# Fused attention and expert block: q in one transfer, 64x64 score tiles, scale chains in PSUM, transposed output, a re-planned order

## The chip, the cores and the metric

One Trainium2 chip, one of its cores. The metric is the device time of the program in microseconds (us), median of three runs. Five engines appear: TensorE (PE for matmuls, PEld for weight loads), VectorE (DVE), ScalarE (ACT), GpSimd (POOL) and SyncE (SP), which issues the transfers.

## The reference

Causal attention over 4 batches of 12 heads, 448 positions, head size 64, then an expert layer with three hidden projections and a maximum over them:

```python
scores = scale * np.matmul(q, k.transpose(0, 1, 3, 2))
scores = np.where(mask, -1000000000.0, scores)
attn = np.exp(scores - max); attn = attn / (sum + 1e-09)
x = np.matmul(attn, v)            # laid out as [4 * 448, 768]
h = np.maximum(np.maximum(x @ w1, x @ w2), x @ w3)
out = h @ w_out                   # [1792, 768], all float32
```

## The kernel before

**Precision.** Score matmuls run in float32. Everything behind them runs in float16 as a high and a low part (`hi`, `lo`), three matmuls per product. The weights arrive as 64-bit floats and are turned into such pairs on the chip.

**Order.** Nothing is issued as written. Functions record operations with `add`, each with engines it may run on, a cost, what it reads and writes, a priority and a ring of buffers; `Order.forward` (L127) places them greedily in planned time, and `Order.run` emits them in that order. So each engine's queue is a fixed list, and an instruction whose data is late holds up all behind it. `W_AT` (L31) says when each of 24 weight tiles is due, `V_AHEAD` when values are loaded. PE has no allowance: an instruction may be planned for the moment at which its data is planned to be ready.

**Attention.** A unit is a pair of heads; there are 24, six per batch. `staging` (L433) loads k as [128, 448] and q as [128, 512] in three transfers: 384 columns, and for the last 64 queries two blocks of 64x64 on the diagonal of a 128x128 square whose rest was set to zero at the start (L866). The tile is scaled by 0.125. `attend` (L453) makes scores in two halves, each in a PSUM tile S (two tiles exist). The first half holds queries 256 to 383 and 0 to 127. The second (from L476) holds 128 to 255 and the last 64 queries of both heads: mask matmuls, then two matmuls over all 128 rows with the zero-padded square as stationary operand (L480, L481; 256 and 192 columns), then two matmuls of 64 rows each, one per head. Row maxima are taken by DVE (L497), exponentials by ACT (L508). The first six pairs ("plain") multiply float32 probabilities with v after PE transposes (L522, L595) and divide at the end (`quotient`, L623). The other 18 scale and split p into halves (L308, L319), transpose them by DMA (L562) and multiply with split v (L582).

**Weights.** `weight` (L655) loads a 768 KB tile, takes the absolute value on ACT (L696), the largest entry (L681) and three bit steps (L685, L689, L693) on DVE; `scales` (L702) makes power-of-two factors for three tiles at a time: `all_max` (L337) spreads the maxima over partitions with a PE matmul into one of three PSUM tiles M, DVE reduces them into `wpm` in SBUF (L347), and four small DVE instructions follow on SBUF tiles (L712, L354, L357, L719). `values` has the same chain once per batch for v. `split` (L730) writes the float16 pair, high part on ACT, POOL or DVE, low part on DVE (L328) or POOL.

**Expert layer.** `hidden` (L765): per batch and per 128 hidden columns, three groups of 18 matmuls of 448 columns (L779), scaled and combined on ACT and DVE (L793), split again. `project` (L816): output rows of 128 tokens by 384 columns, 18 matmuls each with h as stationary operand (L825). The 64 tokens left over per batch are copied by POOL into `hL` (L809), and two batches share a group. There are 28 groups.

The lines of the second half's scores, for the two places that change most:

```python
m(256, 256, qq[:, 384:512], kk[:, 0:256])      # L480
m(768, 192, qq[:, 384:512], kk[:, 256:448])    # L481
```

Of the kernel before, what the change touches and what calls it, by code (L numbers as in the profile page):

```python
# [15 lines left out]
P = 128  # L16
D = 64
# [13 lines left out]
W_AT = [1.0, 1.2, 1.39, 0.71, 0.9, 1.1, 3.11, 3.31, 3.51, 2.35, 3.36, 3.55, 4.66, 4.87, 5.06, 5.85, 4.54, 4.74, 5.34, 5.52, 5.73, 5.27, 6.13, 6.32]  # L31
V_AHEAD = 2

# [6 lines left out]
    "h lo": ("dve", "pool"), "left": ("pool",),  # L40
}
RINGS = dict(
    qr=3, kr=3, acc=2, p32=2, ph=3, pT=2, v16=5, vr=4, w3=3, x=4, wst=2, h=6, hacc=4, osb=2, S=2, O=1, M=3)
# [11 lines left out]
class Order:  # L55
# [14 lines left out]
    WIN = 0  # L70
    WINC = 0
# [55 lines left out]
    def forward(self, prio):  # L127
# [21 lines left out]
        while ready:  # L149
            cand = []  # L150
            for i in ready:
# [22 lines left out]

            limit = s + min(self.WIN, self.WINC * c)
            _, s, i, e, c = min((z[1], z[0], z[2], z[3], z[4]) for z in cand if z[3] == e and z[0] <= limit)
# [81 lines left out]
def attention_moe(ctx: ExitStack, tc: tile.TileContext, q, k, v, w1, w2, w3, wo, out):  # L258
# [8 lines left out]
        qr=([P, 512], F32), kr=([P, S_LEN], F32), acc=([P, 28], F32), p32=([P, 1024], F32), ph=([P, 16, P], F16),  # L267
        pT=([P, 16, P], F16), v16=([P, 2, DM], F16), vr=([P, DM], F32), w3=([P, DM], F32), x=([P, 3, 2, S_LEN], F16), wst=([P, 3072], F16),
        h=([P, 2, S_LEN], F16), hacc=([P, S_LEN], F32), osb=([P, HF], F32))
# [10 lines left out]
    hL = c1.tile([P, KC, 2, P], F16, name="hL")  # L280
    junk = c1.tile([P, DM], F16, name="junk")
    osc = c1.tile([P, 8], F32, name="osc")
    oscL = osc[:, 4:5]
# [5 lines left out]
    wpm = c1.tile([P, 24], F32, name="wpm")  # L289
# [47 lines left out]
    def all_max(name, cols, out, reads, writes, prio):  # L337


        M, n = ("M", "max", name), len(cols)  # L340

# [9 lines left out]
        add([("dve", c_dve(n * P) + 0.06)], mx, reads=[M], writes=writes, prio=prio)  # L351

    def exponent(t, m):
        DVE.tensor_scalar(out=t.bitcast(I32), in0=m.bitcast(I32), scalar1=EXP32, scalar2=None, op0=ALU.bitwise_and)  # L354

    def at_least(t, lo):
        DVE.tensor_scalar(out=t, in0=t, scalar1=2.0**-14, scalar2=lo, op0=ALU.mult, op1=ALU.max)  # L357

# [507 lines left out]
    for t in buf["qr"]:  # L866
        DVE.memset(t[:, 384:512], 0.0)
# [70 lines left out]
```

## Time and profile before

| | |
|---|---|
| runs, median (lowest to highest) | 515.79 us (514.93 to 517.59) |
| the profiled execution, its own time | 514.46 us |
| its span | 512.7 us, TensorE's granted clock 0.983 on average |
| busy: PE, DVE, ACT, POOL | 481.5, 290.6, 303.9, 102.6 us |

The profile gives one execution. Busy time of an engine is the union of its instructions; matmuls are pipelined, so PE counts as busy also while only the tail of a matmul runs. An engine's idle time is shown with what ended it.

### The profile page before, as it was taken

What the parts mean: (1) busy time and instruction counts of PE and PEld (TensorE: products, weight loads), DVE (VectorE), ACT (ScalarE), POOL (GpSimd) and SP (SyncE); (2) the same over time, 40 slices, a digit from 0 to 9 for tenths busy, and PEclk for the clock granted to TensorE, in tenths of its full rate; (3) what the DMA queues carried; (4) which work ended last, traced back from release to release, by engine and by line L of the source; (5) the groups of instructions that cost most, each with busy time, mean ns of one, the idle gap of its engine ahead of it and who ended that gap; (6) DMA issues with size and microseconds to landing.
All of it is one profiled execution on the core that took longest, in us unless ns stands there. A gap on an engine that the chain in (4) does not pass through costs nothing.

```text
span 512.7 us, 9828 instructions
## 1 busy us (share of the span) xinstructions
PE 481.5 (94%) x3882; PEld 288.7 (56%) x3882; DVE 290.6 (57%) x519; ACT 303.9 (59%) x735; POOL 102.6 (20%) x109
## 2 busy tenths in 40 slices
PE   6987868999889898999999999999999999999996
PEld 3766755555555455565665555665555565555563
DVE  3789898999997999997466642422222101111200
ACT  4887777997889788999999952671101111100121
POOL 3111524453144425251125010000000000000000
PEclk9789899999999999999999999999999999999999
DMA  8764635896969789764776502576000010000012
GB/s 247 219 213 133 196 115 178 196 213 169 247 116 207 185 211 245 215 122 56 182 164 123 80 1 57 131 151 97 20 0 1 1 59 35 1 0 1 0 63 61
DMA packets 106797, 60.40 MB, mean 118 GB/s; under 512 B 80640, under 2 KB 104192, under 8 KB 106752
## 3 DMA queue, kind: packets, MB, share of 16 engines
q1 hardware_dynamic: 106752, 59.78, 48.1%
q8 instruction: 30, 0.49, 0.4%
q14 instruction: 15, 0.12, 0.1%
HBM read 35.39 MB, written 5.51 MB: 80 GB/s over the span
## 4 chain that ended last, share of the span: by engine, by line
PE 57%; DVE 23%; ACT 11%; issue 4%; DMA 3%; SPq 1%; ACTq 0%; DVEq 0%
PE M L779 31%; PE M L825 16%; PE S L470 5%; DVE acc L497 4%; ACT p L508 3%; DVE w L689 3%; PE O L582 3%; ACT p L308 3%; DVE w L693 2%; DVE w L328 2%; DMA wst<-in_moe_w_dram 2%; DVE w L681 2%; ACT ph L308 1%; DMA v<-in_v_dram 1%; ACT w L696 1%
## 5 line engine op out<-in xcount | busy, mean ns | idle before, releaser
L779 PE MATMUL M<-x,w 128*128 128x448 f16 x1296 | 251.7, 353 | 2.7 <-DVE w L328 1.6
L779 PEld LDWEIGHTS <-w 128*128 128x128 f16 x1296 | 124.1, 98 | 120.0 <-issue 3.6
L793 DVE SCALAR_TENSOR_TENSOR hacc<-M,wr,hacc 128x448 f32<-128x448 f32 x48 | 32.6, 680 | 115.0 <-PE M L779 114.9
L508 ACT ACTIVATE p<-S,acc 128x384 f32<-128x384 f32 (+3 forms) x168 | 82.6, 500 | 10.0 <-DVE acc L497 3.5
L497 DVE TENSOR_REDUCE acc<-S 128x2 f32<-128x768 f32 (+1 forms) x96 | 62.2, 680 | 19.2 <-PE S L470 17.4
L825 PE MATMUL M<-w,h 128*128 128x384 f16 x432 | 71.9, 326 | 0.0
L470 PE MATMUL S<-kr,qr 64*128 64x384 f32 (+4 forms) x384 | 67.0, 406 | 0.0
L308 ACT ACTIVATE p<-p,acc 128x384 f32<-128x384 f32 (+3 forms) x126 | 58.9, 532 | 12.1 <-DVE acc L538 12.1
L308 ACT ACTIVATE h<-hacc 128x448 f16<-128x448 f32 x24 | 13.6, 573 | 86.8 <-DVE hacc L793 86.8
L825 PEld LDWEIGHTS <-h 128*128 128x128 f16 x432 | 41.6, 98 | 28.7 <-issue 1.3
L809 POOL COPY hL<-h 128x128 f16<-128x128 f16 x24 | 10.2, 427 | 220.9 <-DVE h L319 211.6
L319 POOL TENSOR_TENSOR ph<-p,ph 128x1024 f16<-128x1024 f32 x19 | 42.1, 2216 | 56.2 <-ACT ph L308 28.2
L470 PEld LDWEIGHTS S<-kr,qr 64*128 64x128 f32 (+1 forms) x384 | 40.7, 190 | 18.5 <-issue 10.6
L308 ACT ACTIVATE ph<-p 128x1024 f16<-128x1024 f32 x36 | 37.8, 1051 | 0.7 <-DMA pT<-ph 0.6
L308 ACT ACTIVATE osb<-M,osc 128x384 f32<-128x384 f32 x25 | 14.4, 578 | 36.9 <-PE M L825 36.8
L508 ACT ACTIVATION_READ_ACCUMULATOR p<-S,acc 128x1 f32 x168 | 34.2, 204 | 0.0
L308 ACT ACTIVATE hacc<-M,wr 128x448 f32<-128x448 f32 x24 | 15.0, 627 | 28.0 <-PE M L779 28.0
L319 DVE TENSOR_TENSOR ph<-p,ph 128x1024 f16<-128x1024 f32 x17 | 20.8, 1222 | 16.2 <-ACT ph L308 15.2
L582 PEld LDWEIGHTS <-v 128*64 128x64 f16 x1080 | 26.3, 111 | 5.8 <-issue 5.6
L582 PE MATMUL O<-pT,v 128*64 128x128 f16 (+1 forms) x1080 | 28.3, 210 | 0.0
L470 PE MATMUL S<-mk,identb 128*128 128x128 bf16 (+1 forms) x120 | 17.4, 243 | 10.0 <-ACT p L508 9.7
L689 DVE SCALAR_TENSOR_TENSOR w<-wst,w 128x768 int32<-128x768 int32 x24 | 25.2, 1056 | 0.1
(96 smaller groups left out, 449.5 us busy)
## 6 DMA issues: line engine op xcount, KB each, us to landing
wst<-in_moe_w_dram SPq DMA_DIRECT2D x18, 768.0 KB, 5.7
kr<-in_k_dram SPq DMA_DIRECT2D x24, 224.0 KB, 3.4
qr<-in_q_dram SPq DMA_DIRECT2D x24, 192.0 KB, 3.6
wst<-in_moe_w_out_dram SPq DMA_DIRECT2D x6, 768.0 KB, 4.8
out_dram<-osb SPq DMA_DIRECT2D x24, 192.0 KB, 1.9
vr<-in_v_dram SPq DMA_DIRECT2D x9, 384.0 KB, 3.8
v<-in_v_dram SPq DMA_DIRECT2D x3, 384.0 KB, 3.7
qr<-in_q_dram SPq DMA_DIRECT2D x48, 16.0 KB, 3.3
```

Source lines behind the costliest of these rows:

```text
L308: ACT.activation(o, i, AF.Copy, scale=f)
L319: ENG[eng].tensor_tensor(out=o, in0=i, in1=hi, op=ALU.subtract)
L328: DVE.scalar_tensor_tensor(out=o, in0=i, scalar=f, in1=hi, op0=ALU.mult, op1=ALU.subtract)
L470: PE.matmul(o[:, c : c + w], l, r, start=start, stop=True, skip_group_check=True)
L497: DVE.tensor_reduce(out=T(acc)[:, at : at + len(g)], in_=i, op=ALU.max, axis=AX.XY if parts == 2 else AX.X, negate=True)
L508: ACT.activation(part(T(y), parts, c, w), part(T(S), parts, c, w), AF.Exp, bias=T(acc)[:, at : at + 1], accum_out=T(acc)[:, 7 + at : 8 + at])
L582: PE.matmul(T(O)[D * h : D * h + D, P * i : P * i + w], vt[j][:, vl, (2 * p + h) * D : (2 * p + h + 1) * D], T(pT[u])[:, 8 * pl + c, a : a ...
L681: DVE.tensor_scalar(out=T(x32), in0=T(x32), scalar1=MIN_HI, scalar2=None, op0=ALU.max, op1=ALU.max, accum_out=wmx[:, c])
L689: DVE.scalar_tensor_tensor(out=xi(), in0=word(0), scalar=29, in1=xi(), op0=ALU.logical_shift_right, op1=ALU.bitwise_or)
L779: PE.matmul(T(M)[:, 0:S_LEN], w16[j][:, kk, wl, fs], xx[:, kk % 3, xl], start=(kk == 0 and wl + xl == 0), stop=(kk == 5 and wl == 1))
L793: DVE.scalar_tensor_tensor(out=a, in0=ps, scalar=r, in1=a, op0=ALU.mult, op1=ALU.max)
L825: PE.matmul(T(M)[:, 0:HF], lhs(f, hl), w16[3][:, f, wl, es], start=(f == 0 and hl + wl == 0), stop=(f == 5 and hl == 1))
```

## The change

q is loaded in one transfer of [128, 448] and scaled as it is; there is no square and no clearing of it. The last queries' scores are made by four matmuls, each of 64 rows and 64 output partitions, one head at a time, instead of two over 128 rows. `all_max` becomes `powers`: the reduced maxima and the intermediate results of the scale chain stay in columns 384 and up of the PSUM tile M, which is thus held until the chain's last step but one; only the last results go to SBUF. The projection is transposed: w_out is the stationary operand and h streams, 448 columns at a time, 24 groups of [128, 448]; the output array is [768, 1792], and is turned round on the host outside the measured time. `hL` and its POOL copies are gone. The ring `w3` of weight tiles has four buffers for three. In the planner an instruction of PE planned later than 90 us may start only 1 us (`PAD`) after the data that other engines make for it is planned to be ready; a window rule that was set to nothing is removed; `W_AT` and the first batch's value load (`V_FIRST`) have other due times.

```diff
-W_AT = [1.0, 1.2, 1.39, 0.71, 0.9, 1.1, 3.11, 3.31, ...]
+W_AT = [0.0, 0.7, 0.5, 0.3, 0.0, 1.32, 5.33, 4.23, ...]
+V_FIRST = 13
...
-    qr=3, ..., w3=3, ...
+    qr=3, ..., w3=4, ...
...
+    PAD = 1.0
+    PAD_FROM = 90.0
...
+                    if e == "pe" and t0 > self.PAD_FROM:
+                        t0 = max(t0, self.PAD + max(r0, *(z[1] for z0, z in est[i].items() if z0 != "pe"), 0.0))
...
-    def all_max(name, cols, out, reads, writes, prio):
+    def powers(name, cols, lo, shifted, out, inverse, reads, writes, prio):
         M, n = ("M", "max", name), len(cols)
+        def at(i):
+            return T(M)[:, 384 + n * i : 384 + n * i + n]
...
-                out=out, in_=T(M)[:, 0 : n * P].rearrange("p (a b) -> p a b", b=P), op=ALU.max, axis=AX.X)
+                out=at(0), in_=T(M)[:, 0 : n * P].rearrange("p (a b) -> p a b", b=P), op=ALU.max, axis=AX.X)
+        def power(e):
+            DVE.tensor_scalar(
+                out=at(1).bitcast(I32), in0=at(0).bitcast(I32), scalar1=3, scalar2=TOP2, op0=ALU.logical_shift_left,
+                op1=ALU.bitwise_xor)
+        def exponent(e):
+            k = int(shifted)
+            DVE.tensor_scalar(
+                out=at(k + 1).bitcast(I32), in0=at(k).bitcast(I32), scalar1=EXP32, scalar2=None, op0=ALU.bitwise_and)
+        def at_least(e):
+            DVE.tensor_scalar(out=out, in0=at(int(shifted) + 1), scalar1=2.0**-14, scalar2=lo, op0=ALU.mult, op1=ALU.max)
...
-            ENG[e].dma_start(T(qr)[:, 0:384], q[b, p * P : (p + 1) * P, 0:384])
-            for h in range(2):
-                ENG[e].dma_start(
-                    T(qr)[D * h : D * h + D, 384 + D * h : 448 + D * h], q[b, p * P + D * h : p * P + D * h + D, 384:448])
+            ENG[e].dma_start(T(qr), q[b, p * P : (p + 1) * P, :])
...
-                    m(256, 256, qq[:, 384:512], kk[:, 0:256])
-                    m(768, 192, qq[:, 384:512], kk[:, 256:448])
+                    for one, two in ((0, 1), (1, 0)):
+                        for h, part in ((0, one), (1, two)):
+                            hs, w = slice(D * h, D * h + D), (256, 192)[part]
+                            PE.matmul(
+                                o[hs, 256 + 512 * part : 256 + 512 * part + w], qq[hs, 384:448],
+                                kk[hs, 256 * part : 256 * part + w], start=False, stop=True, skip_group_check=True)
...
-        for e2 in range(2):
+        for e2 in range(KC):
...
-                                T(M)[:, 0:HF], lhs(f, hl), w16[3][:, f, wl, es],
+                                T(M)[:, 0:S_LEN], w16[3][:, f, wl, es], T(("h", b, f))[:, hl],
...
-                    ENG[e].dma_start(out[r0 : r0 + n_, es], T(osb)[p0 : p0 + n_, :])
+                ENG[e].dma_start(out[es, b * S_LEN : (b + 1) * S_LEN], T(osb))
...
-    for t in buf["qr"]:
-        DVE.memset(t[:, 384:512], 0.0)
...
-        values(b, 10 * (u - V_AHEAD) if u else 2.5)
+        values(b, 10 * (u - V_AHEAD) if u else V_FIRST)
```

**Order at the start of SP's queue** (kr and qr are k and q of a pair, wst a weight tile as loaded, v the first batch's values). Before:

```order
L444 DMA kr_64<-in_k_dram 128x448
L439 DMA qr_61<-in_q_dram 128x384
L441 DMA qr_61<-in_q_dram 64x64 x2
L384 DMA v_76<-in_v_dram 128x768
L384 DMA v_77<-in_v_dram 128x768
L384 DMA v_78<-in_v_dram 128x768
L444 DMA kr_65<-in_k_dram 128x448
L384 DMA v_79<-in_v_dram 64x768
L439 DMA qr_62<-in_q_dram 128x384
L441 DMA qr_62<-in_q_dram 64x64 x2
L665 DMA wst_92<-in_moe_w_dram 128x6x256
```

and with the change:

```order
L452 DMA kr_64<-in_k_dram 128x448
L450 DMA qr_61<-in_q_dram 128x448
L677 DMA wst_93<-in_moe_w_dram 128x6x256
L452 DMA kr_65<-in_k_dram 128x448
L450 DMA qr_62<-in_q_dram 128x448
L677 DMA wst_94<-in_moe_w_dram 128x6x256
L398 DMA v_76<-in_v_dram 128x768
L398 DMA v_77<-in_v_dram 128x768
L398 DMA v_78<-in_v_dram 128x768
L452 DMA kr_66<-in_k_dram 128x448
L398 DMA v_79<-in_v_dram 64x768
```

Two weight tiles moved ahead of the values and of the second pair.

**PE's queue at the two score halves of the 16th pair** (S_106 and S_107, with the change S_107 and S_108, are the two score tiles; x and w are the expert layer's operands). Before:

```order
L470 MATMUL S_106<-kr_64,qr_61 128x384 x2
L470 MATMUL S_106<-kr_64,qr_61 128x128 x2
L470 LDWEIGHTS identb
L470 MATMUL S_107<-mk,identb 128x128
L470 LDWEIGHTS identb
L470 MATMUL S_107<-mk,identb 128x128
L470 LDWEIGHTS identb
L470 MATMUL S_107<-mk,identb 128x128
L470 MATMUL S_107<-kr_64,qr_61 128x256
L470 MATMUL S_107<-kr_64,qr_61 128x192
L470 MATMUL S_107<-kr_64,qr_61 128x256 x2
```

and with the change:

```order
L780 LDWEIGHTS w_1_114
L780 MATMUL M_111<-x_92,w_1_114 128x448
L478 LDWEIGHTS identb
L478 MATMUL S_108<-mk,identb 128x128
L478 LDWEIGHTS identb
L478 MATMUL S_108<-mk,identb 128x128
L478 LDWEIGHTS identb
L478 MATMUL S_108<-mk,identb 128x128
L491 MATMUL S_108<-kr_64,qr_61 64x256
L491 MATMUL S_108<-kr_64,qr_61 64x192 x2
L491 MATMUL S_108<-kr_64,qr_61 64x256
L478 MATMUL S_108<-kr_64,qr_61 128x256 x2
```

The two halves stood back to back; now 24 expert matmuls stand between them, and the two full-array matmuls have become four small ones.

**DVE's queue at the first weight scale chain** (w_87 and w_88 are weight tiles, acc the maxima and sums). Before:

```order
L347 TENSOR_REDUCE wpm<-M_111 128x3
L689 SCALAR_TENSOR_TENSOR w_87<-wst_92,w_87 128x768
L712 TENSOR_SCALAR wt<-wpm 128x3
L693 SCALAR_TENSOR_TENSOR w_87<-wst_92,w_87 128x768
L354 TENSOR_SCALAR wt<-wt 128x3
L608 TENSOR_SCALAR acc_67<-acc_67 128x7
L609 RECIPROCAL acc_67<-acc_67 128x7
L357 TENSOR_SCALAR wt<-wt 128x3
```

and with the change:

```order
L349 TENSOR_REDUCE M_112<-M_112 128x3
L309 TENSOR_SCALAR pT_75<-M_110 128x512
L693 TENSOR_SCALAR w_88,wmx<-w_88 128x768
L354 TENSOR_SCALAR M_112<-M_112 128x3
L509 TENSOR_REDUCE acc_67<-S_107 128x2
L697 TENSOR_SCALAR w_88<-w_88 128x768
L360 TENSOR_SCALAR M_112<-M_112 128x3
L701 SCALAR_TENSOR_TENSOR w_88<-wst_94,w_88 128x768
L364 TENSOR_SCALAR wt<-M_112 128x3
```

The chain's middle steps read and write M, and M is free only after the fourth of them instead of after the first.

## Rows read from the trace of the kernel before

**Rows 1.** Windows: stretch, length, busy us (instructions) per engine, PE clock, DMA share, GB/s.

```profile
0.00:84.00 84.00, 68.31 (x625) 51.64 (x626) 66.03 (x136) 60.97 (x163) 24.24 (x38) 0.90 0.60 187
84.00:240.00 156.00, 144.99 (x1331) 85.06 (x1331) 148.51 (x264) 137.56 (x322) 59.77 (x43) 1.00 0.80 184
240.00:508.00 268.00, 268.00 (x1930) 151.95 (x1928) 76.04 (x120) 104.83 (x250) 18.60 (x28) 1.00 0.27 59
508.00:513.00 5.00, 0.21 (x2) 0.00 (x0) 0.00 (x0) 0.58 (x1) 0.00 (x0) 0.99 0.21 49
```

**Rows 2.** Waits of PE between 84 and 240 us: total, times, longest.

```profile
PE S L470 <- ACT p L508: 7.4, 9, 1.6
PE M L779 <- DVE w L328: 1.6, 1, 1.6
```

**Rows 3.** Timeline: the first expert matmuls on PE (start, length us).

```profile
85.37 11.52 PE L779 MATMUL M<-x,w 128*128 128x448 f16 x60
```

**Rows 4.** Windows as in rows 1, the start and the plain pairs.

```profile
0.00:17.78 17.78, 13.38 (x58) 7.83 (x59) 7.45 (x24) 8.99 (x24) 5.11 (x17) 0.81 0.85 267
17.78:80.62 62.84, 52.34 (x550) 41.98 (x549) 55.23 (x111) 49.35 (x131) 18.11 (x20) 0.92 0.56 174
```

**Rows 5.** Timeline of DVE: first score maxima, first weight step, last plain quotient.

```profile
6.50 1.29 DVE L497 TENSOR_REDUCE acc<-S 128x2 f32<-128x768 f32 x2 [4.81 <-PE S L470]
...
17.78 0.93 DVE L681 TENSOR_SCALAR_CACHE_REDUCE w<-w 128x768 f32<-128x768 f32 x1
...
80.62 0.62 DVE L623 TENSOR_TENSOR hacc<-O,hacc 128x448 f32<-128x448 f32 x1
```

**Rows 6.** DMA issues: count, KB each, median us from issue to landing.

```profile
wst<-in_moe_w_dram SPq DMA_DIRECT2D x18, 768.0 KB, 5.7
```

**Rows 7.** Groups by form, DVE: busy us, mean ns of one, idle before.

```profile
L681 DVE TENSOR_SCALAR_CACHE_REDUCE w<-w 128x768 f32<-128x768 f32 x24 | 22.4, 942 | 3.8 <-ACT w L696 3.6
L685 DVE TENSOR_SCALAR w<-w 128x768 int32<-128x768 int32 x24 | 14.6, 617 | 0.1
L693 DVE SCALAR_TENSOR_TENSOR w<-wst,w 128x768 int32<-128x768 int32 x24 | 24.6, 1029 | 0.0
```

**Rows 8.** Groups by form, DVE: the scale chain's three steps on weights.

```profile
L712 DVE TENSOR_SCALAR wt<-wpm 128x3 int32<-128x3 int32 x8 | 5.8, 724 | 0.0
L354 DVE TENSOR_SCALAR wt<-wt 128x3 int32<-128x3 int32 x8 | 3.2, 401 | 0.0
L357 DVE TENSOR_SCALAR wt<-wt 128x3 f32<-128x3 f32 x8 | 3.1, 383 | 0.0
```

**Rows 9.** Timeline: one such step beside POOL work, and the step after it.

```profile
221.77 2.13 POOL L319 TENSOR_TENSOR ph<-p,ph 128x1024 f16<-128x1024 f32 x1 [5.03 <-issue]
...
221.98 1.95 DVE L712 TENSOR_SCALAR wt<-wpm 128x3 int32<-128x3 int32 x1
...
223.96 0.17 DVE L354 TENSOR_SCALAR wt<-wt 128x3 int32<-128x3 int32 x1
```

**Rows 10.** One line's instructions: duration ns min/median/max, first and last start.

```profile
L693 DVE SCALAR_TENSOR_TENSOR w<-wst,w x24: 942/948/2886, 23.6 to 233.9; 128x768 int32<-128x768 int32 x24
```

**Rows 11.** Timeline of PE: a second score half, from narrow windows; then what follows.

```profile
276.85 0.98 PE L470 MATMUL S<-kr,qr 128*128 128x256 f32 x4
...
277.50 0.96 PE L470 MATMUL S<-kr,qr 128*128 128x192 f32 x5
...
277.76 0.49 PE L470 MATMUL S<-kr,qr 64*128 64x256 f32 x2
...
278.39 1.57 PE L582 MATMUL O<-pT,v 128*64 128x128 f16 x60
```

**Rows 12.** Chain of waits, one piece, and timeline of the last two output copies on ACT.

```profile
365.01 44.37 PE M L779 x234
...
505.37 0.58 ACT L308 ACTIVATE osb<-M,osc 128x384 f32<-128x384 f32 x1 [2.35 <-PE M L825]
508.30 0.58 ACT L308 ACTIVATE osb<-M,osc 128x384 f32<-128x384 f32 x1 [2.35 <-PE M L825]
```

More of the change, by code (lines that the diff above doesn't have):

```diff
@@ L448, in scale @@
             scaled(e, T(qr), T(qr), 0.125)
-        add(c_dma((P, 1536), (D, 256), (D, 256)), ld, writes=[qr], ring=("qr", qr), prio=prio)
-        add(c_scaled("q", 512), scale, writes=[qr], prio=prio, port=True)
+        add(c_dma((P, 4 * S_LEN)), ld, writes=[qr], ring=("qr", qr), prio=prio)
+        add(c_scaled("q", S_LEN), scale, writes=[qr], prio=prio, port=True)
     def attend(b, p, prio, plain):
@@ L705, in scales @@
         c, names = slice(3 * f, 3 * f + 3), [("wt", 3 * f + z) for z in range(3)]
-        pm, tt, ff = wpm[:, c], wt[:, c], wf[:, c]
-        all_max(("wt", f, "all"), [wmx[:, 3 * f + z : 3 * f + z + 1] for z in range(3)], pm, [("wmx", 3 * f + z) for z in range(3)],
-                names, prio)
-        def power(e):
-            DVE.tensor_scalar(
-                out=tt.bitcast(I32), in0=pm.bitcast(I32), scalar1=3, scalar2=TOP2, op0=ALU.logical_shift_left,
-                op1=ALU.bitwise_xor)
-        add([("dve", 0.15)], power, writes=names, prio=prio)
-        add([("dve", 0.15)], lambda e: exponent(tt, tt), writes=names, prio=prio)
-        add([("dve", 0.15)], lambda e: at_least(tt, 2.0**-62), writes=names, prio=prio)
-        add([("dve", 0.15)], lambda e: DVE.reciprocal(ff, tt), reads=names, writes=[("wf", 3 * f + z) for z in range(3)], prio=prio)
+        tt, ff = wt[:, c], wf[:, c]
+        powers(("wt", f, "all"), [wmx[:, 3 * f + z : 3 * f + z + 1] for z in range(3)], 2.0**-62, True, tt, ff,
+               [("wmx", 3 * f + z) for z in range(3)], names + [("wf", 3 * f + z) for z in range(3)], prio)
         if f < KC:
@@ L726, in ratios @@
                     out=wr[:, c], in0=tt, scalar1=wtm[:, 6 + f : 7 + f], scalar2=2.0**-18, op0=ALU.mult, op1=ALU.mult)
-            add([("dve", 0.5)], ratios, reads=names, writes=[("wr", f), ("wtm", f)], prio=prio + 1)
+            add([("dve", 0.5)], ratios, reads=names, writes=[("wr", f), ("wtm", f)], prio=prio + 1, port=True)
     def split(m, prio):
@@ L767, in hidden @@
         fs = slice(f * P, (f + 1) * P)
-        free = [("proj", z, t, e2) for z in range(b - (f < RINGS["hacc"] - 1)) for t in range(3) for e2 in range(2)]
+        free = [("proj", z, e2) for z in range(b - (f < RINGS["hacc"] - 1)) for e2 in range(KC)]
         for j in range(3):
@@ L805, in hidden, with project @@
         add(c_rest("h lo", S_LEN), lo, reads=[hacc, (h, 0)], writes=[(h, 1)], prio=EV, port=True)
-        def left(e):
-            ENG[e].tensor_copy(hL[:, f, :, D * (b % 2) : D * (b % 2) + D], T(h)[:, :, 384:448])
-        c = dict(dve=0.15, pool=0.25)
-        add([(e, c[e]) for e in ENGINES["left"]], left, reads=[(h, 0), (h, 1)], writes=[("hL", f)], prio=EV)
     EV = -100
-    def project(rows, lhs, sc, sc_name, names, prio, done=None):
-        for e2 in range(2):
-            M, osb = ("M", "o", rows[0][2], e2), ("osb", rows[0][2], e2)
-            es = slice(e2 * HF, (e2 + 1) * HF)
+    def project(b, prio):
+        for e2 in range(KC):
+            M, osb = ("M", "o", b, e2), ("osb", b, e2)
+            es = slice(e2 * P, (e2 + 1) * P)
             for part in range(3):
@@ L847, in factor @@
                 out=osc[:, b : b + 1], in0=bsc[:, b, 9:10], scalar1=wu[:, 6:7], scalar2=2.0**18, op0=ALU.mult, op1=ALU.mult)
[L848 to L858 removed]
+        add([("dve", 0.25)], factor, reads=[("scale", b), "wu"], writes=[("osc", b)], prio=prio)
+        project(b, prio)
     DVE.memset(junk[:, 0:512], 0.0)
```

66 lines of the change are left out of this document (24 added, 42 removed).

## The prediction

> **What bounds the kernel now.** I read the windows first, because the program has stages with different limits. They show three [rows 1]. From 240 us to 508 us PE is busy for 268.00 of 268.00 us at the full clock, while every other engine has room: there the time is PE's work and nothing else. From 84 to 240 PE is busy 144.99 of 156.00, so 11.0 us are lost; DVE, with 148.51, has almost no room. Up to 84, before the first expert matmul [rows 3], PE is busy 68.31, idle 15.7, at a mean clock of 0.90. At the end 4.8 us of the last window's 5.0 us are without matmuls: last copy and store.
>
> Since the last stage has no hole, a microsecond of PE idle time saved before 240 comes off the end, and one of PE work added after 84 goes onto it wherever PE is the engine waited for. So the question is what PE's idle time does, and what PE's own work does. The waits of PE between 84 and 240 [rows 2] say what the 11.0 us are: 7.4 are score matmuls waiting for exponentials to free their score tile, in nine places, up to 1.6 us each; 1.6 is a wait for the low part of a weight; the rest is small. PE stands still there because its queue is fixed and the score matmul's turn came before its tile was free, not because there was no expert work.
>
> **The change, part by part.** I work against the profiled execution's own 514.46 us and add at the end the 1.3 us by which the median, 515.79, lies above it. About 0.5% (2.6 us) is what a measurement of this kernel can tell from no change.
>
> *Start and plain pairs, up to 84 us.* Two weight tiles now load ahead of the values. DVE begins weight work at 17.78 before, and has been idle for 10.3 of these 17.78 us [rows 4, 5]. With the first weight issued at about 2 us and landing 5.7 us later [rows 6], and a pass of ACT over it for which I set 1 us, it can begin near 8.7; some 4 us of idle time become usable. In exchange more work stands in DVE's queue ahead of the sixth plain quotient, the one that ends at 81 us [rows 5]. Counting there in the two orders, I find ten largest-entry steps for eight and nine each of the three bit steps for eight: 2 x 0.94 + 0.62 + 2 x 1.03, or 4.6 us by their durations [rows 7]. About as much is added and removed in other small steps. The first score maximum, which ran at 6.50 [rows 5], now stands behind the first weight's largest entry and so near 9.5; but its exponentials are no longer behind three sums over v. Usable idle and added work cancel; I take 0, between -4 and +4. The single q transfer and the shorter q scaling save issue slots on SP and time on POOL, which PE hardly waits for: 0.
>
> *Scale chains in PSUM.* The three steps on weights average 724, 401 and 383 ns for 128x3 elements [rows 8], though such a step takes 0.17 us when POOL is quiet; the 1.95 us one ended, at 223.93, within 0.03 us of the POOL instruction that began before it [rows 9]. So the excess is waiting for POOL: eight times 0.55, 0.23 and 0.21, together 7.9 us. With source and result in PSUM I expect the first two steps not to wait, and the third, which writes SBUF, hardly. That is 0 to 7.9 us less on DVE; I take 6. DVE's gain reaches the end only through PE's waits, so it isn't added by itself: it makes the next term likely.
>
> The Trainium skill's page "SBUF — State Buffer", section "Who interferes with whom", says that a DVE instruction in a two-port mode, or one with two SBUF inputs against a POOL instruction that reads SBUF, blocks for the whole of the other. By it the step that follows may block in place of the chain; the first rival below works this out.
>
> *The order at PE, 84 to 240 us.* Of the 11.0 us idle, the allowance of 1 us acts on the 7.4 us of score waits: expert matmuls now stand between two halves that stood back to back. Counting expert matmuls between neighbouring score halves behind the first expert group, I find two gaps with none before and none now, where the smallest is six. Weights come earlier and DVE has some 6 us more room, which serves the 1.6 us wait too. An allowance of 1 us doesn't cover a wait of 1.6 entirely. Lower bound of the gain 0 (waits that move elsewhere), upper bound all 11.0. I take 7.5, nearest to the score waits and a little of the rest.
>
> *The second score half.* Before, the two full-array float32 matmuls run from 276.85 to 277.76, the two per-head ones of 256 columns from there to 278.39 [rows 11]. A full-array matmul costs 4 cycles a column: (256 + 192) x 4 / 2.4 GHz is 0.75 us, of 0.91 shown. The per-head pair takes 0.63 us for two matmuls of 0.43 each, so the two halves of the array work side by side; the gain over 0.85 is plain. The new four matmuls are two such pairs, each holding one of 256 and one of 192 columns. In step, a pair lasts as long as its longer one: 2 x 0.427 = 0.85 us for 0.75, so 0.11 us more. There is also one more change of array shape. In rows 11 the change to half-array matmuls costs 277.76 - 277.50 - 0.16 = 0.10 us; but loading 64 columns of weights instead of 128 gives some back. I take +0.15 us per pair. Eighteen of the 24 pairs lie after 84 us: +2.7 us. The six earlier ones lie in PE's 15.7 idle us [rows 1]; without that cover they would add 0.9. Bounds: +0.05 each (0.9 in all), and the case in which the four run one after another, which is a rival.
>
> The page "TensorEngine Tiling (Array Packing)", section "Key Properties", of the Trainium skill says that a change of tiling mode drains the engine. The 0.10 us above agrees. Taken alone on top of the 0.11 us it makes +0.21 per pair and +3.8 us in the sum; without any cost of the switch it would be +1.9.
>
> *The projection.* 504 matmuls of 384 columns become 432 of 448: both 193,536 columns. Eighteen of the old take 508.30 - 505.37 = 2.93 us, 0.163 each; a 448-column matmul in an unbroken run takes 44.37 / 234 = 0.190 [rows 12]. That is 82.0 us before and 81.9 after: 0. POOL's copies into hL go; after 240 PE has no idle at all, so they cost nothing. At the end one store of 229 KB replaces two smaller ones, the last copy is 448 columns for 384: +0.1, within 0.3 either way.
>
> Sum: 0 - 7.5 + 2.7 + 0 + 0.1 = -4.7, so 509.8 in this execution's terms and **511.1 us** for the median.
>
> **Rivals.**
>
> 1. *The waits only move.* A scale chain now keeps one of three M tiles through four DVE steps with others between them, where only the first held it. Expert groups have two tiles meanwhile; a group takes 18 x 0.19 = 3.4 us, so each of the twelve chains can stall PE if its tile's copy is late, and a chain that doesn't wait for POOL hands the wait to the next weight step, whose longest took 2.89 us for a median of 0.95 [rows 10]. Then the idle time stays near 11 us and only the score cost is left: 515.8 + 2.7, about 518; with half the gain kept, 515. For it: DVE has only 7.5 us of room in the stage. Against it: what follows the blocked step in rows 9 was again a step of the chain, which no longer touches the shared way.
>
> 2. *Slower: the 64x64 matmuls run one after another.* Then each second half pays 2 x 0.75 for 0.75, and a change of shape: +0.85 us on PE. It decides if less than about half of the second matmul of a pair lies beside the first; 18 x 0.85 = 15.3, less 7.5 saved: 515.8 + 7.8, about 524; up to 531 if nothing is saved. For it: the trace has no pair of unequal lengths. Against it: pairs in different halves of the array plainly overlap [rows 11].
>
> 3. *The plain stage grows.* DVE's extra 4.6 us ahead of the sixth quotient isn't paid from idle time, because the first maxima wait for a weight that lands late; expert matmuls start 4 to 5 us later, and half of the later gain is lost: 515.8 + 4.5 - 3.8 + 2.7, about 519.
>
> 4. *Everything pays.* All 11.0 us go and the start gains 4: 515.8 - 11 - 4 + 2.7, about 503.5.
>
> **How the numbers follow.** My forecast (most score waits go, pairs run side by side) gets 0.56, with its own range 506 to 515; rival 1 gets 0.20, rival 2 0.08, rival 3 0.09, rival 4 0.07. The range holds 8 in 10: it takes in the forecast, rival 4 at its edge, rival 1 and most of rival 3, and leaves out rival 2: 504 to 520. Faster means below 513.2: some three quarters of the forecast, 0.43, rival 4, 0.07, and a little of rival 1, 0.03: 0.53. Slower means above 518.4: rival 2, two thirds of rival 3, and a quarter of rival 1: 0.19. The rest, 0.28, is the same.
>
> **What would show it.** In the changed profile, PE idle between its first expert matmul and about 240 us should be near 3.5 us, with the score waits on exponentials near 1 us in all; steps of the chain with M as source should take 0.2 us, also beside POOL; a second half should take about 1.7 us from its first score matmul to what follows, with pairs starting together; PE's first expert matmul should stand within 4 us of 85. If PE waits appear on M tiles (for DVE's chain or the copies of expert groups), rival 1 holds; second halves of 2.3 us and more mean rival 2; a first expert matmul at 89 or later, rival 3. The prediction is wrong if the last stage shows PE idle at all, or if PE's busy time grows by more than 5 us.

## The result, and the profile after

| | before | with the change |
|---|---|---|
| median (lowest to highest) | 515.92 us (514.93 to 517.59) | 507.94 us (507.28 to 509.1) |
| the profiled execution, its span | 514.46 us, 512.7 us | 507.28 us, 505.6 us |
| busy: PE, DVE | 481.5, 290.6 us | 481.3, 280.3 us |

The ratio is 0.9836, with a 95% interval of 0.9806 to 0.9866: 8.0 us or 1.6% faster. The forecast was 511.1 with a range of 504 to 520, so the direction and the range held, and the gain was forecast too small, 4.7 for 8.0. Measured again beside later experiments, the changed kernel took 508.69 us (508.38 to 509.82), ratio 0.9860, interval 0.9842 to 0.9878. The mean granted clock differs between executions, but it doesn't make the gain: of 33 executions of the kernel before, the six with a mean of 0.986 to 0.992 have a median span of 513.7 us, and the changed kernel's four, at 0.986 to 0.993, have 506.2.

The windows of the changed kernel, in the columns of [rows 1] and nearly the same stretches:

```profile
0.00:84.00 84.00, 70.19 (x666) 48.74 (x667) 72.22 (x150) 62.91 (x163) 20.62 (x36) 0.94 0.61 196
84.00:240.00 156.00, 149.31 (x1350) 86.14 (x1349) 136.12 (x244) 139.76 (x332) 66.79 (x44) 1.00 0.77 182
240.00:501.00 261.00, 261.00 (x1893) 141.31 (x1894) 71.99 (x113) 101.03 (x241) 12.50 (x10) 1.00 0.25 59
```

PE's idle time is the length of a stretch less its busy time. Up to 84 us it went from 15.7 to 13.8, from 84 to 240 from 11.0 to 6.7, and the last stage has no hole as before. In a second profile of the changed kernel (the run beside later experiments) it is 15.1 and 6.4: what was saved up to 84 us lies between 0.6 and 1.9. DVE works 136.1 us of the middle stage for 148.5: it has 20 us of room there instead of 7.5.

PE's waits between 84 and 240 us, which answer to [rows 2]:

```profile
PE S L478 <- ACT p L520: 4.8, 5, 1.5
PE O L594 <- DVE v L327: 1.5, 1, 1.5
```

Score matmuls still wait, in five places instead of nine, and a wait on a converted value tile took the place of the one on a weight tile. No expert matmul waits for an M tile.

The first expert matmuls on PE (compare [rows 3]), and DVE's first weight step with the first score maxima behind it (compare [rows 5]), from the timeline:

```profile
80.84 4.71 PE L780 MATMUL M<-x,w 128*128 128x448 f16 x24
87.04 0.33 PE L478 MATMUL S<-mk,identb 128*128 128x128 bf16 x3 [1.48 <-ACT p L520]
```

```profile
8.51 0.95 DVE L693 TENSOR_SCALAR_CACHE_REDUCE w<-w 128x768 f32<-128x768 f32 x1 [7.24 <-ACT w L708]
...
9.38 1.28 DVE L509 TENSOR_REDUCE acc<-S 128x2 f32<-128x768 f32 x2
```

The first expert matmul comes 4.5 us earlier in this execution. That is not a head start of 4.5 us: a second score half of 1.8 us, which begins at 87.04 here, stood ahead of the expert work before and now stands behind its first 24 matmuls. After the same work PE is 2.7 us earlier, and 1.3 in the second profile, where the first expert matmul comes at 82.28. DVE's weight work starts at 8.5 us instead of 17.8, and the first maxima at 9.4 instead of 6.5, both as expected.

DVE's groups by form, the low halves of before first, then those of the changed kernel, which answer to [rows 7, 8] (L354, L360, L364 are the three chain steps; L327, before L328, makes low halves of weights; L697, L701, L705 are the bit steps):

```profile
L328 DVE SCALAR_TENSOR_TENSOR w<-w,wf,w 128x768 f16<-128x768 f32 x24 | 23.7, 1021 | 0.5 <-POOL w L312 0.4
```

```profile
L327 DVE SCALAR_TENSOR_TENSOR w<-w,wf,w 128x768 f16<-128x768 f32 x24 | 29.8, 1273 | 0.0
L705 DVE SCALAR_TENSOR_TENSOR w<-wst,w 128x768 int32<-128x768 int32 x24 | 27.0, 1134 | 0.0
...
L697 DVE TENSOR_SCALAR w<-w 128x768 int32<-128x768 int32 x24 | 16.7, 708 | 0.0
...
L360 DVE TENSOR_SCALAR M<-M 128x3 int32<-128x3 int32 x8 | 1.3, 161 | 0.0
L354 DVE TENSOR_SCALAR M<-M 128x3 int32<-128x3 int32 x8 | 1.3, 157 | 0.0
L364 DVE TENSOR_SCALAR wt<-M 128x3 f32<-128x3 f32 x8 | 1.2, 152 | 0.0
```

The chain steps fell from 12.1 us to 3.8, all of what I had called waiting for POOL. But the low halves grew from 23.7 to 29.8, and of the bit steps L705 from 24.6 to 27.0 and L697 from 14.6 to 16.7, while L701 fell from 25.2 to 22.4. This looks like the first rival; the experiment on the chains tells whose work it is.

A second score half on PE: the mask matmuls, the eight instructions of the four 64x64 matmuls, the per-head ones, and what follows:

```profile
272.86 0.33 PE L478 MATMUL S<-mk,identb 128*128 128x128 bf16 x3
273.12 0.97 PE L491 MATMUL S<-kr,qr 64*64 64x256 f32 x8
274.03 0.70 PE L478 MATMUL S<-kr,qr 64*128 64x256 f32 x4
274.66 0.36 PE L780 MATMUL M<-x,w 128*128 128x448 f16 x1
```

and the mask matmuls ahead of the half that [rows 11] show, in the kernel before:

```profile
276.68 0.33 PE L470 MATMUL S<-mk,identb 128*128 128x128 bf16 x3
```

From the first 64x64 matmul to the per-head ones it is 274.03 - 273.12 = 0.91 us, what the two full-array matmuls took, 277.76 - 276.85. The only difference stands ahead: 273.12 - 272.86 = 0.26 us from the masks to the first score matmul, for 0.17 before.

The last output copy:

```profile
501.90 0.64 ACT L307 ACTIVATE osb<-M,osc 128x448 f32<-128x448 f32 x1 [2.77 <-PE M L819]
```

From its start to the end of the span it is 3.7 us; before, from 508.30 [rows 12] to 512.7, it was 4.4. The one store is issued at 502.56, right behind the copy; before, the second of two was issued at 509.4, 0.5 us behind it.

Summed over PE, the span of 512.7 us became 505.6: 1.9 us less idle up to 84 us, 4.3 less in the middle stage, 0.7 less at the end, 0.2 less busy. In the second profile, of 506.7 us, it is 0.6, 4.6, 0.7 and nothing.

### The profile page after: what moved, and what is told of

The parts are those of the page before. It is cut to its first block, busy times and chain, and to the rows that moved or that the text cites. A ratio compares the mean times of both kernels' runs of the same rounds, so it can differ in the third digit from the quotient of the medians.

```text
span 505.6 us, 9706 instructions
## 1 busy us (share of the span) xinstructions
PE 481.3 (95%) x3906; PEld 276.4 (55%) x3906; DVE 280.3 (55%) x506; ACT 304.3 (60%) x733; POOL 99.9 (20%) x89
## 4 chain that ended last, share of the span: by engine, by line
PE 60%; DVE 18%; ACT 15%; DMA 4%; issue 3%; SPq 0%; DVEq 0%; ACTq 0%
PE M L780 32%; PE M L819 16%; PE S L478 4%; ACT p L520 4%; DVE acc L509 3%; DVE w L705 3%; PE O L594 3%; ACT w L307 3%; DVE w L701 3%; ACT p L307 3%; DMA wst<-in_moe_w_dram 2%; DVE w L327 2%; PE S L491 2%; ACT ph L307 2%; ACT w L708 2%
## 5 line engine op out<-in xcount | busy, mean ns | idle before, releaser
L780 PEld LDWEIGHTS <-w 128*128 128x128 f16 x1296 | 124.1, 98 | 117.5 <-issue 4.2
L819 PE MATMUL M<-h,w 128*128 128x448 f16 x432 | 83.6, 353 | 0.0
L318 POOL TENSOR_TENSOR ph<-p,ph 128x1024 f16<-128x1024 f32 x23 | 53.1, 2309 | 68.6 <-issue 36.4
L819 PEld LDWEIGHTS <-w 128*128 128x128 f16 x432 | 41.5, 98 | 39.4 <-issue 1.0
L478 PE MATMUL S<-kr,qr 64*128 64x256 f32 (+2 forms) x288 | 46.6, 430 | 0.0
L307 ACT ACTIVATE osb<-M,osc 128x448 f32<-128x448 f32 x24 | 15.2, 632 | 38.8 <-PE M L819 38.8
L478 PEld LDWEIGHTS S<-kr,qr 64*128 64x128 f32 x288 | 25.0, 195 | 19.6 <-issue 13.5
L307 ACT ACTIVATE hacc<-M,wr 128x448 f32<-128x448 f32 x24 | 15.1, 628 | 26.0 <-PE M L780 26.0
L327 DVE SCALAR_TENSOR_TENSOR w<-w,wf,w 128x768 f16<-128x768 f32 x24 | 29.8, 1273 | 0.0
L708 ACT ACTIVATE w<-wst 128x768 f32<-128x768 f32 x24 | 21.9, 912 | 11.1 <-DMA wst<-in_moe_w_dram 7.0
L318 DVE TENSOR_TENSOR ph<-p,ph 128x1024 f16<-128x1024 f32 x13 | 15.9, 1224 | 22.7 <-ACT ph L307 22.7
L693 DVE TENSOR_SCALAR_CACHE_REDUCE w<-w 128x768 f32<-128x768 f32 x24 | 22.6, 944 | 10.2 <-ACT w L708 10.2
```

Source lines behind the costliest of these rows:

```text
L307: ACT.activation(o, i, AF.Copy, scale=f)
L318: ENG[eng].tensor_tensor(out=o, in0=i, in1=hi, op=ALU.subtract)
L327: DVE.scalar_tensor_tensor(out=o, in0=i, scalar=f, in1=hi, op0=ALU.mult, op1=ALU.subtract)
L478: PE.matmul(o[:, c : c + w], l, r, start=start, stop=True, skip_group_check=True)
L693: DVE.tensor_scalar(out=T(x32), in0=T(x32), scalar1=MIN_HI, scalar2=None, op0=ALU.max, op1=ALU.max, accum_out=wmx[:, c])
L708: add([("act", c_act(DM))], lambda e: ACT.activation(T(x32), word(1).bitcast(F32), AF.Abs), reads=[st], writes=[x32], ring=("w3", x32), pr ...
```

## The experiments

Line numbers are those of each kernel. Where the text says that the order is kept, every engine's instructions stand in the changed kernel's order, so that one thing alone differs. Elsewhere the planner laid out a new order, and the experiment contains that order too.

**Scale chains back in SBUF, order kept.** All chains first:

```diff
         def at(i):
-            return T(M)[:, 384 + n * i : 384 + n * i + n]
+            return out if i else wpm[:, 3 * name[1] : 3 * name[1] + 3] if shifted else bsc[:, name[1], 8:9]
```

> The changed kernel with the scale chains' intermediate values in SBUF again, every queue's order the same, and M held as long as in the changed kernel. Theory (waiting for POOL is saved by PSUM only in part, for the weight step behind takes some of it over): chain steps back to 0.4 to 0.7 us on average, 5 to 8 us more there, but the weight steps (low halves, last two bit steps) some 3 to 6 us shorter; DVE busy up by 2 to 5; the time up by 0 to 2: 508 to 510. Rival 1 of the prediction in pure form (the waits only move): DVE busy and time the same within 1 us. Rival (the full 6 to 8 us are real and PE waits for them): 511 to 513.

Measured: 512.75 us, ratio 0.9933 (0.9908 to 0.9959), 4.8 above the changed kernel, in the range of the last case. But its profile had the first expert matmul 3.5 us later already, with a mean clock of 0.83 over the first 40 us, so part of the loss might be the start's. So the changed kernel and a version with only the eight weight chains in SBUF were run side by side.

> The changed kernel once more, unaltered, beside the next three: with the first four experiments its first expert matmul came at 83.8 to 84.6 us where PE's order up to there was the same, against 80.8 in its own profile. If the 80.8 belongs to the kernel: again 80 to 82 and 507 to 509. If it depends on the execution (the first weight's arrival, the early clock): 83 to 85 in some profiles, and the time still 507 to 510.

Measured: 508.69 us; the first expert matmul came at 82.28. So the 80.8 belongs to one execution. In four profiles with the same queue of PE up to there (these two and those of the two versions on the allowance below) the first expert matmul comes at 80.8 to 83.8 us: this stage varies by up to 3 us.

```diff
         def at(i):
-            return T(M)[:, 384 + n * i : 384 + n * i + n]
+            return T(M)[:, 384 + i : 385 + i] if not shifted else out if i else wpm[:, 3 * name[1] : 3 * name[1] + 3]
```

> The changed kernel with only the eight weight chains' values in SBUF; the values' chains stay in PSUM, and every queue's order is the same. Theory (small DVE steps held behind POOL's long instructions delay what DVE hands to PE): 2 to 5 us above the unaltered kernel beside it, DVE's chain steps 5 to 6 us longer in all. Rival (the loss of the version with all chains in SBUF lay in its start, which varies by execution): within 1 us of the unaltered kernel, although DVE's steps are as much longer.

Measured: 512.02 us, ratio 0.9920 (0.9901 to 0.9939), 3.3 above the unaltered kernel beside it; the intervals don't overlap. A part may be the clock: the unaltered kernel's four executions have a mean of 0.988 to 0.990, and against them the three of this version at 0.987 to 0.989 have a median of 511.23, 2.5 above. One step of the chain in this version, with POOL's instruction beside it (timeline):

```profile
140.06 2.70 POOL L318 TENSOR_TENSOR ph<-p,ph 128x1024 f16<-128x1024 f32 x1 [3.71 <-issue]
```

```profile
140.69 2.09 DVE L360 TENSOR_SCALAR wt<-wt 128x3 int32<-128x3 int32 x1
142.70 0.61 DVE L327 SCALAR_TENSOR_TENSOR x<-O,x 128x448 f16<-128x448 f32 x1
```

and the same step in the unaltered kernel:

```profile
138.52 2.62 POOL L318 TENSOR_TENSOR ph<-p,ph 128x1024 f16<-128x1024 f32 x1 [3.73 <-issue]
```

```profile
139.07 0.15 DVE L360 TENSOR_SCALAR M<-M 128x3 int32<-128x3 int32 x1
139.14 0.61 DVE L327 SCALAR_TENSOR_TENSOR x<-O,x 128x448 f16<-128x448 f32 x1
```

In SBUF the step of 128x3 elements lasts 2.09 us, to 142.78, and POOL's subtraction ends at 142.76. In PSUM it lasts 0.15 us in the middle of the same subtraction, and the step behind it doesn't wait either: it is no longer a chain step but one that makes x, which the whole pair needs. DVE's groups of the version with SBUF chains:

```profile
L327 DVE SCALAR_TENSOR_TENSOR w<-w,wf,w 128x768 f16<-128x768 f32 x24 | 29.9, 1280 | 0.0
L705 DVE SCALAR_TENSOR_TENSOR w<-wst,w 128x768 int32<-128x768 int32 x24 | 26.8, 1125 | 0.0
...
L697 DVE TENSOR_SCALAR w<-w 128x768 int32<-128x768 int32 x24 | 15.1, 638 | 0.0
L354 DVE TENSOR_SCALAR wt<-wpm 128x3 int32<-128x3 int32 x8 | 4.3, 542 | 0.0
L360 DVE TENSOR_SCALAR wt<-wt 128x3 int32<-128x3 int32 x8 | 4.3, 539 | 0.0
L364 DVE TENSOR_SCALAR wt<-wt 128x3 f32<-128x3 f32 x8 | 1.3, 158 | 0.0
```

Two of three steps wait (0.54 us for 0.16), 6.1 us in all; the third doesn't in this order. L327 and L705 are as long as in the changed kernel: their growth belongs to the order, not to the chains. Only L697 is shorter, by 1.6 us. So about a quarter of the saved waiting moves on (1.6 of 6.1), and the rest is real work of DVE saved. The middle stage of the unaltered kernel:

```profile
84.00:240.00 156.00, 149.62 (x1347) 86.39 (x1347) 137.18 (x246) 140.06 (x333) 66.30 (x43) 1.00 0.74 180
```

and of the one with the chains in SBUF:

```profile
84.00:240.00 156.00, 147.95 (x1332) 85.10 (x1331) 140.96 (x247) 138.73 (x328) 64.72 (x43) 1.00 0.73 177
```

PE's idle time is 6.4 and 8.1 us, and the first expert matmul of the second came 1.05 us later: 2.7 of the 3.1 us between the spans, though the 1.05 is within what the start varies by.

The Trainium skill's page "SBUF — State Buffer", section "Who interferes with whom", says that an instruction of DVE with at most one SBUF input, outside the two-port modes, doesn't contend with POOL. The rows agree: 0.15 us with PSUM as source and result, 2.09 us with both in SBUF. Which mode the step ran in, no row shows.

**The allowance at PE.** Set to nothing, then to a quarter; new orders.

```diff
-    PAD = 1.0
+    PAD = 0.0
```

> The changed kernel with the allowance at PE set to 0 (the planner lays out a new order; everything else as in the changed kernel). Theory (allowance and early weights share the middle stage's gain of 4.3 us): score waits on exponentials between the first expert matmul and 240 us go from 4.8 back to 7 to 9 us, time 510 to 512. Rival (the due times did it all, the allowance nothing): within 1 us of 507.9. Rival (the allowance costs as much as it saves): 505 to 507.

Measured: 511.6 us, ratio 0.9908 (0.9880 to 0.9937).

> The changed kernel with an allowance at PE of 0.25 us (new order by the planner). Theory (the allowance of 1 us is what keeps score matmuls from waiting): score waits 7 to 9 us behind the first expert matmul and 510 to 512, like the version without allowance. Rival (the allowance itself is worth little; the version without it lost by the order that it fell into): 506.5 to 509.

Measured: 510.43 us (507.76 to 511.79), ratio 0.9889 (0.9864 to 0.9915). PE's score waits between 84 and 240 us, and its middle stage with 7.3 us idle, without allowance:

```profile
PE S L478 <- ACT p L520: 7.1, 6, 2.2
```

```profile
84.00:240.00 156.00, 148.74 (x1277) 85.41 (x1276) 135.60 (x246) 133.92 (x309) 51.57 (x34) 0.99 0.71 175
```

and with a quarter:

```profile
PE S L478 <- ACT p L520: 4.2, 7, 1.4
```

```profile
84.00:240.00 156.00, 151.06 (x1348) 86.83 (x1347) 140.10 (x252) 135.50 (x320) 50.95 (x34) 1.00 0.75 177
```

Without allowance the score waits are 7.1 us, as the theory said. With a quarter they are 4.2, no more than with the whole (4.8 and 4.4 in its two profiles), and PE is idle 4.9 us in the middle and 0.9 behind. So 1 us of allowance does not make shorter waits than 0.25, which the theory expected at 7 to 9, and between any two of the three the order changed as well. Medians rise as the allowance falls, 508.7, 510.4, 511.6, but the interval of the quarter overlaps that of the whole. What the allowance is worth by itself, from nothing to some 3 us, stays open.

**The due times.** Put back into the changed kernel, and put alone into the kernel before; new orders.

```diff
-W_AT = [0.0, 0.7, 0.5, 0.3, 0.0, 1.32, 5.33, 4.23, ...]
-V_FIRST = 13
+W_AT = [1.0, 1.2, 1.39, 0.71, 0.9, 1.1, 3.11, 3.31, ...]
+V_FIRST = 2.5
```

> The changed kernel with the old due times of weights and of the first values (planner lays out a new order, with allowance, four weight tiles and all else kept). Theory (the start's gain comes from two weight tiles loaded first, so that DVE works earlier): first expert matmul at 84 to 87 us instead of 80.8, time 510.5 to 513. Rival (the start's gain comes from the single q transfer, the PSUM chain and the higher clock): first expert matmul at 80 to 82, time 507 to 509.

Measured: 542.79 us, ratio 1.0518 (1.0490 to 1.0546). None of my cases. PE has seven score waits of 25.1 us in all, the longest 8.9, and its first expert matmul at 95.5. The old due times don't fit the new structure; why they cost 35 us was not followed, and the run says nothing of what the start gained.

> The kernel before with nothing changed but the due times of weights and of the first values (planner lays out a new order; three weight tiles, square, SBUF chains, no allowance, old projection). Question: is the earlier start of the expert work the due times' alone? If so: first weight step on DVE near 9 us, first expert matmul at 80 to 83 us; the total is then 510 to 520, for the due times were not made for this structure. If it also takes the fourth weight tile, the single q transfer or the PSUM chains: first expert matmul at 84 or later.

Measured: 514.29 us, ratio 0.9975 (0.9948 to 1.0002). Its first expert matmuls, and its windows up to 240 us:

```profile
79.34 2.44 PE L779 MATMUL M<-x,w 128*128 128x448 f16 x12
85.29 0.38 PE L470 MATMUL S<-mk,identb 128*128 128x256 bf16 x2 [3.50 <-ACT p L508]
```

```profile
0.00:84.00 84.00, 65.83 (x623) 48.60 (x624) 75.50 (x152) 60.83 (x155) 21.60 (x33) 0.94 0.62 196
84.00:240.00 156.00, 149.02 (x1304) 87.61 (x1304) 144.90 (x254) 139.55 (x330) 60.68 (x44) 0.99 0.74 176
```

The due times alone bring the first expert matmul forward by 6.0 us, more than the whole change does, but not PE's work. After twelve expert matmuls PE waits 3.50 us for exponentials, and then runs two score halves that stood ahead of the expert work in the kernel before; it is back at expert work at 89.97. Up to 84 us DVE has worked 75.5 us for 66.0, yet PE has done 623 instructions for 625 and is idle 18.2 us for 15.7. The middle stage has 7.0 us idle for 11.0, and 3.2 us of score waits stand in the last stage, where the kernel before has none. In all the due times save at most 2.7 us by the interval, perhaps nothing. The earlier weights pay only with the rest.

**The last queries.** The old square and its three transfers in the changed kernel, order kept (with a smaller scratch tile to make room):

```diff
-            ENG[e].dma_start(T(qr), q[b, p * P : (p + 1) * P, :])
+            ENG[e].dma_start(T(qr)[:, 0:384], q[b, p * P : (p + 1) * P, 0:384])
+            for h in range(2):
+                ENG[e].dma_start(T(qr)[D * h : D * h + D, 384 + D * h : 448 + D * h], ...)
...
-                    for one, two in ((0, 1), (1, 0)):
...
+                    m(256, 256, qq[:, 384:512], kk[:, 0:256])
+                    m(768, 192, qq[:, 384:512], kk[:, 256:448])
```

> The changed kernel with the old last queries: three transfers per q tile, the zero-padded square, two matmuls over 128 rows; every engine's order is kept as in the changed kernel. Theory (the 64x64 matmuls of unequal length run independently, 0.90 us from the first to the per-head pair that follows, as the two full-array ones did; only 0.09 us more ahead of them): PE busy falls by about 24 x 0.09 = 2 us at most, 0.7 to 1.5 of it behind the first expert matmul, and the 48 more transfers and longer q scaling cost 0 to 1: 506.5 to 508.5 against 507.9. Rival (my prediction's 0.15 per pair): 505 to 506. Rival (the 64x64 form is itself a gain): 509 or more.

Measured: 509.07 us, ratio 0.9876 (0.9848 to 0.9903), 0.4 to 1.1 above the changed kernel's two medians, within their intervals; the last case, a gain of the 64x64 form itself, isn't borne out by so little. Its profile had a late start (first expert matmul at 84.61, mean clock 0.83 up to 40 us, as in the version with all chains in SBUF), so its total says little about the transfers. The cheaper second halves show: PE is busy 479.8 us for 481.3, and a second half lasts 277.79 - 276.08 = 1.71 us from its masks to what follows, for 274.66 - 272.86 = 1.80.

```profile
276.08 0.33 PE L481 MATMUL S<-mk,identb 128*128 128x128 bf16 x3
...
277.79 0.55 PE L779 MATMUL M<-x,w 128*128 128x448 f16 x2
```

Then the four small matmuls were paired by equal length:

```diff
-                    for one, two in ((0, 1), (1, 0)):
+                    for one, two in ((0, 0), (1, 1)):
```

> The changed kernel with the four 64x64 matmuls paired by equal length (both heads' 256 columns, then both heads' 192), same order of everything else. Theory (each of the four small matmuls runs on its own quarter of the array as soon as that quarter is free, so only the sum of 448 columns counts): block again 0.90 us, time within 1 us of the unaltered kernel. Rival (pairs go in step): 0.1 us per pair less, 18 x 0.1, so 1.5 to 2 us faster. Rival (both heads writing the same PSUM columns at once hinder each other): 0.3 us and more per pair, 5 us slower.

Measured: 508.4 us, ratio 0.9847 (0.9828 to 0.9866). A second half of it:

```profile
274.35 0.33 PE L478 MATMUL S<-mk,identb 128*128 128x128 bf16 x3
274.61 0.97 PE L491 MATMUL S<-kr,qr 64*64 64x256 f32 x8
275.51 0.70 PE L478 MATMUL S<-kr,qr 64*128 64x256 f32 x4
```

0.90 us for the block, 0.26 ahead of it, the same as with unequal pairs. Pairs of equal length can't lose by going in step, so unequal pairs lose nothing either. The rows fit the theory that each matmul goes on when its own part of the array is free.

**What bounds the start.** The first weight's largest entry behind the first two maxima on DVE, all else in order:

```diff
-        for _, _, i, e in self.placed:
+        order = [(i, e) for _, _, i, e in self.placed]
...
+        order.remove((first, "dve"))
+        order.insert(order.index((self.tag["max", 0, 0, 0, 1], "dve")) + 1, (first, "dve"))
+        for i, e in order:
             ops[i]["emit"](e)
```

> The changed kernel with one DVE instruction moved: the first weight's largest entry stands behind the first two score maxima instead of ahead of them; all else in the same order. Theory (the plain stage is bound by DVE's queue in the changed kernel, which is busy nearly without a gap from 20 us on): the two maxima run in idle time at 7 us instead of 9.4, DVE and the first exponentials are 1.2 to 2 us earlier, the first expert matmul too, and the time is 506.5 to 507.5, 1 to 1.5 below the unaltered kernel's 508. Rival (another limit, transfers or exponentials further on, sets the stage): 507.8 to 508.7, first expert matmul within 0.5 us of 82.

and, in addition, the absolute maximum of the first value tile on ACT:

```diff
+        k = order.index((self.tag["sum", 0, 0], "dve"))
+        order[k] = (self.tag["sum", 0, 0], "act")
```

> As the version with the first maxima moved, and the first values' absolute maximum taken by ACT instead of DVE (one instruction of 0.95 us on DVE, some 0.9 on ACT). Theory (DVE's queue bounds the plain stage): another 0.5 to 1 us earlier, 505.5 to 507. Rival (ACT's exponentials set it as much): the same as or slower than the version with the maxima alone, 507 to 508.5.

Measured: 509.32 us, ratio 0.9866 (0.9845 to 0.9886), and with the values' maximum on ACT 507.98, ratio 0.9847 (0.9829 to 0.9864): both the same as the unaltered kernel. The first exponential, the weight's first bit step, the second half's maxima and the first 40 us, unaltered:

```profile
11.11 0.58 ACT L520 ACTIVATE p<-S,acc 128x384 f32<-128x384 f32 x1 [2.29 <-DVE acc L509]
```

```profile
10.93 0.71 DVE L697 TENSOR_SCALAR w<-w 128x768 int32<-128x768 int32 x1
11.56 1.27 DVE L509 TENSOR_REDUCE acc<-S 128x2 f32<-128x512 f32 x2
```

```profile
0.00:40.00 40.00, 29.91 (x222) 18.92 (x222) 29.34 (x61) 26.56 (x70) 9.52 (x23) 0.91 0.81 257
```

with the maxima first, and POOL's instruction beside the bit step:

```profile
8.89 0.56 ACT L526 ACTIVATE p<-S,acc 128x384 f32<-128x384 f32 x1
```

```profile
10.01 1.75 DVE L703 TENSOR_SCALAR w<-w 128x768 int32<-128x768 int32 x1
11.69 1.27 DVE L514 TENSOR_REDUCE acc<-S 128x2 f32<-128x512 f32 x2
```

```profile
9.98 1.37 POOL L399 MEMSET v<- 64x1536 f16 x1
```

The first exponential runs 2.2 us earlier, but the head start ends on DVE itself: the bit step lasts 1.75 us for 0.71, beside a POOL instruction that began just ahead of it and clears a value tile, and the second half's maxima begin at 11.69 us for 11.56. By 40 us PE and DVE have done as many instructions as without the move, 222 and 61, at the same mean clock. So the move didn't make DVE's queue earlier, and its miss says little about my theory. Without the values' maximum DVE's queue is shorter by 0.95 us; the first expert matmul then came at 82.1 us, with the move alone at 81.3, for 82.3, within what this stage varies by. Whether DVE's queue bounds the plain stage stays open.

## Why the prediction was right, and where its sum was off

The sum was -4.7 us; the spans of the two profiled executions differ by 7.1. The medians differ by 8.0, since the profiled execution of before lies 1.5 below its median and the later one 0.7 below its own. The direction was right, and so was the main reason, less idle time of PE in the middle stage. That the sum came so near was in part luck, for the largest term was put 3 us too high, and the start, the second halves and the end, each put too unfavourably, made up for it.

- **Start and plain pairs, taken as 0.** Too low, and the reason, "usable idle and added work cancel", was half right. DVE up to the end of the sixth quotient, before:

```profile
0.00:81.24 81.24, 66.34 (x609) 50.16 (x611) 63.30 (x133) 58.34 (x154) 23.21 (x37) 0.89 0.62 193
```

and in the changed kernel:

```profile
0.00:78.89 78.89, 65.08 (x637) 46.04 (x637) 67.44 (x141) 57.80 (x153) 18.51 (x34) 0.94 0.60 194
```

DVE's work ahead of that quotient grew by 4.1 us, where I had counted 4.6. Its idle time fell from 17.9 to 11.5 us, where I had counted on 4. The difference, 2.4 us, is what the quotient gains; in the second profile it ends at 80.33, 0.9 us earlier. PE's idle time up to 84 us fell by 0.6 to 1.9, and its mean clock there rose from 0.90 to 0.94. That is inside my -4 to +4. The first expert matmul stands 4.2 and 2.7 us from 85, where I had set 4. That new due times alone raise DVE's early work is shown by the kernel before with them; that they alone save PE anything up to 84 us is not.

- **Scale chains in PSUM, 6 us on DVE.** Right in kind, and measured at 8.3. I gave it no own place in the sum and let it work through the next term. With the order kept it is worth 3.3 us, or 2.5 at like clocks, the largest share that an experiment shows apart from a new order.

- **The order at PE, -7.5.** This is the term that failed most: the idle time fell by 4.3, and the score waits ended at 4.8 us, not at 1. From the first expert matmul to 240 us PE is idle 6.7 us, not 3.5. I gave the credit to the allowance. The experiments give 1.7 us of it to the chains, with the order kept; new due times alone took the idle time of this stage from 11.0 to 7.0, but left 3.2 us of waits behind it; and the allowance's own share isn't told apart from the orders that came with it. How the 4.3 us divide stays open. The longest score wait with an allowance of 1 us is still 1.5 us, so the exponentials come later against PE's queue than planned, by more than the allowance; why was not tried.

- **The second score half, +2.7.** Too much. The change of array shape costs 0.26 - 0.17 = 0.09 us, as the 0.10 in the working. The 0.11 for unequal pairs in step did not come; equal pairs take the same 0.90 us. At 18 x 0.09 it is 1.6. A second half takes 274.66 - 273.12 = 1.54 us from its first score matmul to what follows, not 1.7. The page "TensorEngine Tiling (Array Packing)", section "Key Properties", of the Trainium skill lists beside the drain that I used that tiles operate independently; the block of 0.91 us for 0.91 agrees, and with it the term would have been right.

- **Projection and end.** PE's busy time is the same within 0.2 us although the second halves cost more; the plain pairs' products with v, the same in number, took 13.0 us for 15.7 in the start with its higher mean clock, which covers it. The projection's matmuls take 83.6 us for 84.1. The end saved 0.7 us where I had put +0.1: one store of the last tile instead of two outweighs the longer copy, 0.5 us of it by the second store's later issue.

Of the rivals, the first (waits only move) holds for about a quarter of the chains' waiting, and no expert matmul waited for an M tile. The second and third are refuted by the rows of the second half and of the first expert matmul. Of the fourth neither half came in full: 0.6 to 1.9 us of idle time in the start where it had 4 us, and 4.3 of 11 in the middle stage. The result lies between it and the forecast.

## What to carry to other kernels

Look for tiny instructions that last much longer than their size: when their excess ends together with another engine's instruction, giving them operands in PSUM takes them out of the way; here 6.1 us of waiting were worth 2.5 to 3.3 at the end. An earlier start is worth only what the stages behind it can take up, and the first instruction of the next stage doesn't measure it, since a new order can put work behind it: compare after the same work; due times fitted to one structure can be worth nothing or do harm in another. Where a term rests on work side by side that the trace doesn't show, take the form that the shown pairs have, with the bound for the range.

## What the runs showed of the hardware

- A DVE step of 128x3 elements took 2.09 us with source and result in SBUF while POOL subtracted in SBUF, and 0.15 us in PSUM beside the same instruction. A bit step of 128x768 elements took 1.75 us where it began 0.03 us behind the start of a POOL instruction that clears a tile, and 0.71 us in another version, 1.08 us behind it.
- Four matmuls of 64 rows and 64 columns, of 256 and 192 columns of data, took 0.90 to 0.91 us however they were paired, as long as the two full-array ones that do the same with a half of zeros. The change to this shape cost 0.09 us.
- TensorE's mean granted clock in the start differs between executions of one kernel: 0.88 and 0.91 up to 40 us in the changed kernel's two profiles. In the versions with all chains in SBUF and with the old square it was 0.83. The first of these:

```profile
0.00:40.00 40.00, 30.50 (x212) 19.64 (x214) 26.94 (x55) 25.32 (x69) 9.04 (x23) 0.83 0.79 254
```

By 40 us PE had then done 212 instructions for 222, and the first expert matmul came at 84.4 us, with the square at 84.6. A difference of 2 to 3 us in the total of two versions of this kernel can lie there.
